# A fused attention and MLP kernel: near keys first, summary keys in rows 96 to 119, and V's means by products for pairs 0 and 1

## The chip, the cores and the metric

The kernel runs on one core of a Trainium2 chip. The metric is the device time of one execution in microseconds (us); the profile of one execution gives the span from the first to the last instruction. Engines are named as in the profile: PE (TensorE matmul), PEld (its weight loads), DVE (VectorE), ACT (ScalarE), POOL (GpSimd), and SP, on whose queue every DMA is issued.

## The reference, cut to what matters

Two batches, 8 heads, 768 positions, head size 64. Each query attends to keys less than 16 positions away and to 24 summary keys, one for each block of 32 positions; the output feeds two MLP layers.

```python
k_sum = k.reshape(B, H, nb, block, D).max(axis=3)       # block = 32, nb = 24
v_sum = v.reshape(B, H, nb, block, D).mean(axis=3)
mask_l = np.abs(pos[:, None] - pos[None, :]) < window   # window = 16
scores_s = scale * np.einsum('bhsd,bhnd->bhsn', q, k_sum) + np.log(block)
a = softmax(concatenate([where(mask_l, scores_l, -1e9), scores_s]))
x = a @ concatenate([v, v_sum])
h = relu(x @ w_in); u, v = halves of h; v_n = normalise(v)
x = (u * (w_spatial @ v_n + b_spatial)) @ w_out
h = relu(x @ w_in2); out = (h * sigmoid(conv3(h))) @ w_out2
```

## The kernel before

Heads go in pairs: 8 pairs, numbered 0 to 7 (0 to 3 are batch 0). A pair's 768 queries are 12 blocks of 64, and six blocks make a group, so there are 16 groups, two to a pair. A block sees 94 near keys (`WK`, 64 and 15 on each side) and 24 summary keys, `NK` = 118 columns; the summaries stand in columns and rows 0 to 23, the near keys behind them.

A group goes through these steps, by function and line. `keys` copies scaled near keys into `kws` (`win`, L393/L395, one for each group), takes block maxima on DVE (`top`, L403, two halves for pairs 0 to 3) and puts them beside the near keys (`put`, L409). `group` writes logarithms, masks and scores into PSUM (`qk`, L483, L489, L499), takes the row maximum on DVE (L503), six exponentials on ACT (`exps`, L509), sum and reciprocal on DVE (L512, L515), normalises on POOL or DVE (L518), transposes three blocks at a time on PE (L522, two halves h0 and h1, copied by L545), multiplies by V (`pv`, L528) and writes two parts of the result (L550, L551). Two score buffers alternate, so the scores of group i+2 wait for the exponentials of group i. The result of `pv` and the transpose in `means` share the bank `xp`.

`means` gives the 24 means of V for a pair, into rows 0 to 23 of the V tile `vws` for all blocks (`put`, L455 on ACT, L457 on POOL or DVE). For pairs 0 and 2 (`MEANS_F`, `MEANS_PE`) they come from 24 products of the V windows with a matrix of 1/32 (L424), which needs zeros in rows 0 to 23 first (L828). For the other pairs V is loaded a second time in another layout (L377, 384 KB), summed on DVE (L445) and transposed on PE (L448).

The matmuls of the dense layers (`mm3`, three products for each, L310 to L312) fill PE between and after the groups. The order of all work is written out by hand: each `add` makes a numbered unit with a cost and its readers and writers, `ORDER` lists the unit numbers, two characters each, in the order of issue, and `PICK` names the engine of each unit that has a choice. Each engine and the SP queue run their units in that order. Where the planner's costs leave PE a gap of 0.5 us or more before the dense stage, it puts in fill matmuls on constants (`warm`, L768); `WARM` of them also stand at the start.

The first DMAs in the queue before are, in order: keys of pair 0 (two halves), queries of pair 0 (first half), keys of pair 1 (two halves), a part of w_in, queries of pair 0 (second half), another part of w_in, queries of pair 1 (first half), V windows of group 0, keys of pair 2 (first half), queries of pair 1 (second half), keys of pair 2 (second half), V windows of group 1. PE's order before, with qk, T (transposes), pv and the group's number: qk0, 6 fill, qk1, 5 fill, qk2, means of pair 0 (first 12 products), qk3, T0h0, means of pair 0 (last 12), T0h1, qk4, T1h0, pv0, T1h1, qk5, T2h0, pv1, qk6, T2h1, means of pair 1 (transpose), dense, T3h0, qk7, T3h1, pv2, T4h0, means of pair 2 (24 products), T4h1, and so on.

Of the kernel before, what the change touches and what calls it, by code (L numbers as in the profile page):

```python
# [11 lines left out]
F32 = mybir.dt.float32  # L12
# [13 lines left out]
WK = QB + 2 * HK  # L26
VK = QB + 32
NS = S // 32
NK = WK + NS
GB = 6  # L30
GA = GB // 2
NG = NB // GB
MK = 5 * WK + 2 * QB + GA * NS
DIRECT = ()
MEANS_F = (0,2)
# [7 lines left out]
MEANS_PE = (0,2)  # L43
# [11 lines left out]
    "AAABACADAGAjAEAhAFAHAkAiAIAlArAMBZANBbBcBaATAsAUAJA4BdAVAWAXA5AaAbAOAYAtBjAcAdAeAfAgAuAKAmBFAvAwBkCUA6A7APA8BGCVCTCSCWAL"  # L55
    "A9BwBxAxAyB9DKBHBlBmAnAoApBnAzAZBoCcB+A0DLDMCdByA+DIAqAQA1A-BeBABBBzDJA2A3B0B1BICpBSCqB-CeCfARCgC2CAChBpBCBDBEDSBqBrBsBf"
    "DxCrDTCsEhCtBgEfB2B3BTDfDgBhCECFBiCuB4B5BtBuBvCiCjBLBMEiBJCXDUDVDhBKCYBNCZBOBPBUCGBVBWCkASClB6B7CaCHCIB8DWC3EoEpCvCwEgCJ"
    "CbDXBQDsCmCnEqCBDNCxE1BXCyBRDYCoCzDyDZDaDiCCEVDjEUFPC0C1DtDkFOCDCLDOE2DbDlDBC4DPDQCKDzBYDuDmDnFNFQDRErEsEtDcEjFWDdC6C7De"
    "C8C9C+DoEuDpDqDrE3FjE4EvEwEkCMC-DACND0DvDCD1COCPCQDwFkFlFwFCFDC5D7D8D9D2D+D-DDF7F8DEDFDGCRDHD3GnGlFmExFnFXD4D5E5D6EFEGEH"
    "EIF9EAE6F+GmEYEaElGoEZEJFGEbEcFYFHFIFJEBECEDEmFKEdFZEEE7E8EPEQERESEnGRFLEeETFMGEGFGSEyE9EWFRFaEzEKELGGHSEMENHTF0GTF1FbE+"  # L60
    "FcE0E-FxGuG7GHF2F3F4EOHIGeFEGfFdFeHJFAGgGhGiFBF5FSGjF6GkHKHLFoG8GvGIGJHUFTFfFpHMHcFVFUHVHWHdHeHNHOHmFqFrHnEXFgHXGUFFGwG9"
    "FsF-FhFyHYHZGxGKHoFiHpJ6HPGyHqGLHfGVGWFtGMHgIjH6FuGNHwGXG+FvGAHhHrHaGzHxHyHzGYGZGBGDGCGOH7H8HQHRH0GaGPGQGbG0GpHsIuH9G-Gc"
    "GdGqG1G2HtHAHuHiIOG3FzIPIQGrGsHBG4HCIzHDLVI0I1IkHbH+GtH1G5G6HEHFHGJ9LOH2HvH-H3HjHkHHIvHlIbITIEIAIUIBICIlIeIfIJImInIRH4H5"
    "IoISIgJwIKIVIhILIwIMJSJTLQLPIcIDIYIdIWIXIZINIaIFIGIHIIIpJUJVIxI4IqI5LcJIJcI2JdI+I3JJLRIrIsI6I7ItJeJfI-IiI8JKJLJWJXJMJNJ7"
    "KIJAI9JgJhJOJPJBJCJDJEJFJmKcKdKeKfKgIyJQJRJnJxJiJjJyJoKhJzKJJpJGJHJqJYJZLSKwKmKSJ0KnJrJsK6K7J1JkJlKxJ+J8LEJ-KyKALFKzKBKT"
    "JaJtLTJbJuJ2J3LXJ4LUJvLWLjLYKCKKK8LZLeLaJ5KiLbKjLdLqKLKoLfLgKULGKpKDKELlKFKMLhLiLkKVKWKXKYKNKOKZKqK0LmKaLnKPM2K9K+LHKbK-"
# [11 lines left out]
)  # L78
PICK = (
    "001111110101011000111110111000000011000001101110001001000011111011000011000101010010101110011001001101001000011011100121"  # L80
    "0210001000100001102200001000010101000100000010000000000000000000000000200200200000200200200200"
)
WARM = 9

# [840 lines left out]
```

## Time and profile before

| what | value |
|---|---|
| median of 3 runs | 333.08 us (332.96 to 333.38) |
| the profiled execution | 333.22 us |
| its span | 331.4 us (1.8 us lie around it) |
| PE busy | 325.2 us, 98% of the span |
| DVE, ACT, POOL busy | 237.1, 186.2, 62.8 us |

Busy time of PE is no measure of its use alone, because the ends of matmuls are modelled; starts are recorded, so the distance from one start to the next tells what PE did.

### The profile page before, as it was taken

The numbers are of one execution on the slowest core, as the hardware profiler recorded it, in microseconds if no ns is written. First come the engines' busy times: TensorE is split into PE (matmuls) and PEld (weight loads), VectorE is DVE, ScalarE is ACT, GpSimd is POOL, SyncE is SP. The second block draws the span as 40 slices with busy tenths as digits, with TensorE's granted clock in tenths as the row PEclk, the third lists the DMA queues.
The fourth block names the chain that finished last, engine by engine and source line by source line (L and its number), as shares of the span: only waits on it lengthen the run. The fifth ranks groups of instructions, "written<-read, shape, count | busy, mean of one in ns | idle before, by whom it ended". The sixth has DMA issues, their size and how long they took to land.

```text
span 331.4 us, 6183 instructions
## 1 busy us (share of the span) xinstructions
PE 325.2 (98%) x2388; PEld 269.0 (81%) x2388; DVE 237.1 (72%) x453; ACT 186.2 (56%) x460; POOL 62.8 (19%) x84
## 2 busy tenths in 40 slices
PE   7999999999999999999999999999999999999996
PEld 3678788878788888889988888888888888888886
DVE  8998888887781457889998597899897975480000
ACT  3988879957533643434441465867877854460111
POOL 6695944533112053001000100000000000000000
PEclk9999999999999999999999999999999999999999
DMA  7998697542046600232523230330000000000101
GB/s 234 312 277 273 181 270 256 163 121 66 7 128 200 199 0 0 65 127 76 161 83 119 73 101 26 128 110 19 0 2 32 32 34 32 32 32 34 63 32 65
DMA packets 13325, 34.49 MB, mean 104 GB/s; under 512 B 1648, under 2 KB 3952, under 8 KB 13296
## 3 DMA queue, kind: packets, MB, share of 16 engines
q1 hardware_dynamic: 13296, 34.10, 32.6%
q8 instruction: 19, 0.31, 0.4%
q14 instruction: 10, 0.08, 0.1%
HBM read 30.95 MB, written 3.15 MB: 103 GB/s over the span
## 4 chain that ended last, share of the span: by engine, by line
PE 94%; DVE 3%; POOL 1%; issue 1%; ACT 1%; DVEq 0%; ACTq 0%; POOLq 0%
PE late L310 12%; PE late L311 12%; PE late L312 12%; PE mm L310 9%; PE mm L311 9%; PE mm L312 9%; PE xp L528 4%; PE pt L522 4%; PE xp L310 3%; PE xp L311 3%; PE xp L312 3%; PE pt L312 3%; PE pt L311 3%; PE pt L310 3%; PE s L499 2%; PE mm L424 1%
## 5 line engine op out<-in xcount | busy, mean ns | idle before, releaser
L716 DVE SCALAR_TENSOR_TENSOR v<-v,conv_t 128x767 f32<-128x767 f32 x32 | 32.5, 1016 | 10.9 <-ACT v L713 10.5
L509 ACT ACTIVATE a<-s,a 128x118 f32<-128x118 f32 x96 | 33.1, 387 | 1.9 <-DVE a L503 1.8
L294 ACT ACTIVATE a<-a 128x512 f32<-128x512 f32 (+1 forms) x28 | 17.7, 640 | 16.2 <-DVE w L279 7.1
L509 ACT ACTIVATION_READ_ACCUMULATOR a<-s,a 128x1 f32 x96 | 22.5, 234 | 0.0
L299 DVE SCALAR_TENSOR_TENSOR a<-a,a 128x512 uint32<-128x512 uint32 (+1 forms) x32 | 19.9, 621 | 2.7 <-ACT a L294 1.2
L518 POOL TENSOR_TENSOR a<-a,a 128x708 f32<-128x708 f32 x14 | 19.1, 1367 | 12.5 <-ACT tmp L589 8.1
L301 DVE SCALAR_TENSOR_TENSOR a<-a,a 128x512 uint32<-128x512 uint32 (+1 forms) x32 | 20.0, 624 | 1.1
L310 PE MATMUL late<-xh,a 128*128 128x512 f32 x48 | 18.7, 389 | 0.0
L311 PE MATMUL late<-xl,a 128*128 128x512 f32 x48 | 18.7, 389 | 0.0
L312 PE MATMUL late<-xh,a 128*128 128x512 f32 x48 | 18.7, 389 | 0.0
L719 ACT ACTIVATE v<-v 128x768 f32<-128x768 f32 x16 | 13.5, 843 | 9.1 <-DVE v L716 9.1
L722 DVE TENSOR_TENSOR v<-v 128x768 f32<-128x768 f32 x16 | 15.1, 955 | 3.3 <-ACT v L719 2.9
L522 PE MATMUL pt<-ident,a 128*118 128x128 f32 x96 | 16.7, 282 | 0.5 <-POOL a L518 0.4
L757 ACT COPY tmp<-late 128x512 f32<-128x512 f32 x7 | 4.1, 589 | 23.0 <-PE late L312 23.0
L279 POOL TENSOR_TENSOR w<-a,w 128x256 fp32r<-128x256 f32 (+1 forms) x11 | 9.6, 881 | 33.5 <-ACT w L285 33.3
L713 ACT ACTIVATE v<-v,conv_t 128x768 f32<-128x768 f32 x16 | 15.0, 940 | 0.6 <-DVE w L279 0.2
L528 PEld LDWEIGHTS xp<-a,a 118*64 118x64 f32 x384 | 12.5, 137 | 3.5 <-issue 2.4
L545 ACT COPY a<-pt 118x384 f32<-118x384 f32 x22 | 10.6, 481 | 7.7 <-PE pt L522 7.4
L503 DVE TENSOR_REDUCE a<-s 128x6 f32<-128x708 f32 x16 | 13.9, 880 | 1.4 <-PE s L499 1.2
L528 PE MATMUL xp<-a,a 118*64 118x64 f32 x384 | 14.7, 226 | 0.0
L310 PE MATMUL mm<-xh,w 128*128 128x256 f32 (+1 forms) x40 | 14.3, 358 | 0.0
L522 PEld LDWEIGHTS pt<-ident,a 128*118 128x118 f32 x96 | 10.5, 136 | 4.6 <-issue 1.2
(337 smaller groups left out, 1016.3 us busy)
## 6 DMA issues: line engine op xcount, KB each, us to landing
a<-w_in SPq DMA_DIRECT2D x12, 512.0 KB, 3.6
a<-w_out SPq DMA_DIRECT2D x8, 512.0 KB, 3.6
out<-tmp SPq DMA_DIRECT2D x11, 256.0 KB, 2.0
a<-vwin SPq DMA_DIRECT2D x8, 288.0 KB, 6.0
a<-v_in SPq DMA_DIRECT2D x6, 384.0 KB, 5.9
a<-vwin SPq DMA_DIRECT2D x4, 576.0 KB, 6.1
tmp<-w_spT SPq DMA_DIRECT2D x6, 384.0 KB, 3.6
a<-w_in SPq DMA_DIRECT2D x8, 256.0 KB, 5.4
```

Source lines behind the costliest of these rows:

```text
L294: mul = {"ACT": (0.2 + n / 1080, lambda: ACT.mul(fu.f(), half(1).bitcast(F32), 2.0 ** -112)), "POOL": (0.12 + n / 1050, lambda: POOL.tenso ...
L299: add({"DVE": (0.16 + n / 960, lambda: DVE.scalar_tensor_tensor(out=last.u(), in0=fu.u(), scalar=0x80000000, in1=last.u(), op0=ALU.bitwise ...
L301: add({"DVE": (0.16 + n / 960, lambda: DVE.scalar_tensor_tensor(out=fu.u(), in0=fu.u(), scalar=3, in1=last.u(), op0=ALU.logical_shift_left ...
L310: PE.matmul(ps, lhsT=lh, rhs=rh, start=first and i == 0, stop=False)
L311: PE.matmul(ps, lhsT=lh, rhs=rl, start=False, stop=False)
L312: PE.matmul(ps, lhsT=ll, rhs=rh, start=False, stop=last and i == n - 1)
L509: ACT.activation(out=e[:, u, :NK], in_=sv[:, u // GA, u % GA], func=AF.Exp, bias=st[:, 0, u:u + 1], scale=SCALE if direct else 1.0, accum_ ...
L518: eng.tensor_tensor(out=e, in0=e, in1=st[:, 1].unsqueeze(2).to_broadcast([128, GB, NK]), op=ALU.mult)
L522: PE.transpose(pt3[:NK, a], e[:, GA * h + a, :NK], ident)
L528: PE.matmul(po[h * D:(h + 1) * D, k * QB:(k + 1) * QB], lhsT=vw3(j)[:NK, g * GB + k, h * D:(h + 1) * D], rhs=pts[:NK, at:at + QB], start=T ...
L716: DVE.scalar_tensor_tensor(out=ct.f()[:, to], in0=hh.f()[:, of], scalar=conv_t[:, 3 * f + k:3 * f + k + 1], in1=ct.f()[:, to], op0=ALU.mul ...
L722: eng.tensor_tensor(out=ct.f(), in0=hh.f(), in1=ct.f(), op=ALU.mult)
```

## The change

The columns and rows are turned round: near keys in 0 to 95 (`WK` becomes 96, two of them zero and masked), summaries in 96 to 119, so `NK` is 120. Key DMAs bring 800 columns for 798, in cuts of 416 and 384. The products for the means read rows 0 to 95 alone, so the zeros (L828) and the second way by a matrix `comb` (L826) go. Pairs 0 and 1 now take their means by products; pair 2 loads V again, and sums and transposes it as pairs 3 to 7 do. The logarithm is spread over 64 rows (`ones` on the left), which drops the constants `three` and `many`; inner masks are one tile read three times. The tile `one` is made on ACT (`one_tile`) and no longer on DVE. Planner costs change, `WARM` is 7, and `ORDER` and `PICK` are new.

By the new tables PE has as many units as before (515), ACT 286 for 281, DVE 393 for 399, POOL 74 for 74. The first DMAs are: keys of pair 0 (second half, then first), a part of w_in, queries of pair 0 (first half), keys of pair 1 (two halves), queries of pair 0 (second half), another part of w_in, queries of pair 1 (first half), V windows of group 0, keys of pair 2 (two halves), queries of pair 1 (second half), V windows of group 1. PE's order is: qk0, 3 fill, qk1, 7 fill, qk2, means of pair 0 (first 12), qk3, T0h0, means of pair 0 (last 12), T0h1, qk4, T1h0, pv0, qk5, T1h1, means of pair 1 (24 products), T2h0, pv1, T2h1, qk6, T3h0, pv2, T3h1, qk7, T4h0, pv3, two dense units, T4h1, means of pair 2 (transpose), qk8, T5h0, pv4, T5h1, T6h0, pv5. Both orders have done the same work at the end of T8h1. PE changes its way of tiling 50 times before and 51 times after.

```diff
-WK = QB + 2 * HK
-VK = QB + 32
+WK = QB + 32
-MEANS_F = (0,2)
+MEANS_F = (0,1)
-MEANS_PE = (0,2)
-WARM = 9
+WARM = 7
...
-            dma((k1 - k0) / 2, lambda k0=k0, k1=k1: SP.dma_start(kt(n).ap[:, k0:k1], k_in[b, p][:, k0:k1]), r - 12 + 0.5 * i, writes=[kt(n).tok(k0, k1)])
+            dma((k1 - k0) / 2 * (1.07 if kp == 2 else 1.0) - (90 if n + i == 0 else 0), lambda k0=k0, k1=k1: SP.dma_start(kts[n % 2].ap[:, k0:k1], k_in[b, p][:, k0:k1]), r - 12 + 0.5 * i, writes=[kts[n % 2].tok(k0, k1)])
...
-            dma(48 * (b1 - b0), lambda b0=b0, b1=b1: SP.dma_start(vw3(j)[NS:NS + VK, b0:b1], vwin[b, p][:, b0:b1]), r - 6 + 0.5 * i,
+            dma(52 * (b1 - b0), lambda b0=b0, b1=b1: SP.dma_start(vw3(j)[:WK, b0:b1], vwin[b, p][:, b0:b1]), r - 6 + 0.5 * i,
...
-                dst = kw3(j)[:, g * GB:(g + 1) * GB, NS:]
+                dst = kw3(j)[:, g * GB:(g + 1) * GB, :WK]
...
-                        PE.matmul(ps, lhsT=runs_t.ap[:NK, NZ - 2 * blk:NZ - 2 * blk + NS], rhs=vw3(j)[:NK, blk], start=blk == 0, stop=blk == NB - 1)
-                add({"PE": (1.41, mm)}, r + 1 + 0.5 * g, [vw_tok(j, g, "w"), vw_tok(j, g, "m"), runs_t.tok()], [m], mode="F")
+                        PE.matmul(ps, lhsT=runs_t.ap[:WK, NZ - 2 * blk:NZ - 2 * blk + NS], rhs=vw3(j)[:WK, blk], start=blk == 0, stop=blk == NB - 1)
+                add({"PE": (1.41, mm)}, r + 1 + 0.5 * g, [vw_tok(j, g, "w"), runs_t.tok()], [m], mode="F")
...
-                dst, src = vw3(j)[:NS, g * GB:(g + 1) * GB], vss[j].ap[:NS].unsqueeze(1).to_broadcast([NS, GB, 128])
+                dst, src = vw3(j)[WK:NK, g * GB:(g + 1) * GB], vss[j].ap[WK:NK].unsqueeze(1).to_broadcast([NS, GB, 128])
...
-                    PE.matmul(sv[c * QB:(c + 1) * QB, h, :, :NS], lhsT=(many if direct else three)[rows], rhs=logs[rows].rearrange("p (a k) -> p a k", k=NS),
+                    PE.matmul(sv[c * QB:(c + 1) * QB, h, :, WK:], lhsT=ones[rows, :QB], rhs=logs[rows].rearrange("p (a k) -> p a k", k=NS),
...
+    def one_tile():
+        for h, rows in enumerate(halves):
+            ACT.copy(one[rows], ident[rows, h * QB:(h + 1) * QB])
     def mask_tiles():
-        for h, rows in enumerate(halves):
-            DVE.tensor_copy(one[rows], ident[rows, h * QB:(h + 1) * QB])
         DVE.tensor_copy(tiles[:, 0], tiles[:, 1])
-        DVE.tensor_copy(tiles[:, 2:], tiles[:, 1].unsqueeze(1).to_broadcast([128, 3, WK]))
+        DVE.tensor_copy(tiles[:, 2:], tiles[:, 1].unsqueeze(1).to_broadcast([128, 2, WK]))
...
-    add({"DVE": (0.2, lambda: DVE.tensor_reduce(out=comb.ap, in_=ident.rearrange("p (j r) -> p r j", r=32)[:, :NS], op=ALU.add, axis=AX.X))}, -97, [tok("ident")], [comb.tok()])
-    for j in sorted({n % 2 for n in MEANS_PE}):
-        add({"POOL": (1.4, lambda j=j: POOL.memset(vws[j].ap[:NS], 0.0)), "DVE": (0.85, lambda j=j: DVE.memset(vws[j].ap[:NS], 0.0))}, -98, writes=[vws[j].tok(sub="m")], lock=True)
+    add({"ACT": (2.65, one_tile)}, -99, [tok("ident")], [mask_b.tok(sub="o")])
+    add({"DVE": (0.55, mask_tiles)}, -99, [tok("ident")], [mask_b.tok(sub="m")], lock=True)
```

## Rows read from the trace of the kernel before

**Rows 1.** The page: busy shares in 40 slices of 8.3 us.
```profile
PE   7999999999999999999999999999999999999996
```

**Rows 2.** Busy time by stage; ends with clock, DMA share and GB/s.
```profile
8.00:20.00 12.00, 11.55 (x207) 8.02 (x209) 10.92 (x25) 10.51 (x53) 8.65 (x12) 1.00 1.05 312
```

**Rows 3.** The timeline of the first 14 us, the start; start, duration, engine, line.
```profile
2.79 1.37 POOL L828 MEMSET a<- 24x1536 f32 x1
2.99 1.44 DVE L798 CAST a<-ident 64x64 bf16<-64x64 f32 x2
...
5.25 0.53 DVE L403 TENSOR_REDUCE a<-a 128x12 f32<-128x384 f32 x1
...
5.92 0.67 ACT L393 ACTIVATE a<-a 128x564 f32<-128x564 f32 x1 [2.12 <-DMA a<-k_in]
6.50 0.31 DVE L409 TENSOR_SCALAR a<-a 128x288 f32<-128x288 f32 x1
...
7.00 0.43 SPq L371 DMA_DIRECT2D a<-q_in  x1
7.13 0.45 ACT L294 ACTIVATE a<-a 128x256 f32<-128x256 f32 x1 [0.53 <-DMA a<-w_in]
```

**Rows 4.** PE's timeline from 5 to 60 us, the first groups.
```profile
6.91 0.84 PE L499 MATMUL s<-a,a 64*64 64x118 f32 x24 [1.32 <-DVE a L409]
...
13.45 0.23 PE L483 MATMUL s<-a 64*64 64x72 bf16 x4
...
14.85 0.54 PE L522 MATMUL pt<-ident,a 128*118 128x128 f32 x3 [0.45 <-POOL a L518]
15.32 1.49 PE L424 MATMUL mm<-a,a 118*24 118x128 f32 x12
...
23.02 0.54 PE L522 MATMUL pt<-ident,a 128*118 128x128 f32 x3
23.65 0.28 PE L448 MATMUL xp<-ident,a 128*24 128x128 f32 x1
```

**Rows 5.** ACT's timeline: exponentials of groups 0, 1, 2 and 6, first of each.
```profile
8.73 0.36 ACT L509 ACTIVATE a<-s,a 128x118 f32<-128x118 f32 x1 [1.16 <-DVE a L503]
...
11.04 0.36 ACT L509 ACTIVATE a<-s,a 128x118 f32<-128x118 f32 x1
...
13.62 0.39 ACT L509 ACTIVATE a<-s,a 128x118 f32<-128x118 f32 x1
...
27.00 0.37 ACT L509 ACTIVATE a<-s,a 128x118 f32<-128x118 f32 x1
```

**Rows 6.** DMA issues of the queries, line L371.
```profile
DMA to landing us min/median/max: 3.7/5.8/8.2
```

**Rows 7.** The chain that ended last, 18 to 30 us: start, duration, what.
```profile
23.04 0.57 DVE xl L551
...
24.17 0.11 PE mm L312
...
24.37 0.52 PE pt L522 x3
24.89 0.16 PE s L483 x4
...
25.19 0.31 PE s L489 x4
25.51 0.60 PE s L499 x24
...
26.58 0.85 PE xp L528 x24
```

**Rows 8.** POOL's timeline: normalising and putting.
```profile
21.69 2.69 POOL L518 TENSOR_TENSOR a<-a,a 128x708 f32<-128x708 f32 x2
24.36 0.65 POOL L395 TENSOR_SCALAR a<-a 128x564 f32<-128x564 f32 x1
...
33.03 0.82 POOL L457 TENSOR_SCALAR a<-a 24x768 f32<-24x768 f32 x1
```

More of the change, by code (lines that the diff above doesn't have):

```diff
@@ L186, in u, with bf16_parts @@
         return self.ap.bitcast(U32)
-def bf16_parts(x, k):
-    out, kind = [], mybir.dt.np(BF16)
-    for _ in range(k):
+def bf16_parts(x, times):
+    kind = mybir.dt.np(BF16)
+    out = [float(np.float32(x / times).astype(kind))]
+    x -= times * out[0]
+    for _ in range(2):
         out.append(float(np.float32(x).astype(kind)))
-        x = np.float32(x) - np.float32(out[-1])
+        x -= out[-1]
     return out
@@ L408, in put @@
         def put(eng):
-            eng.tensor_scalar(out=kw3(j)[:, :, :NS], in0=ks.ap[:, :NS].unsqueeze(1).to_broadcast([128, NB, NS]), scalar1=SCALE, scalar2=0.0,
+            eng.tensor_scalar(out=kw3(j)[:, :, WK:], in0=ks.ap[:, :NS].unsqueeze(1).to_broadcast([128, NB, NS]), scalar1=SCALE, scalar2=0.0,
                               op0=ALU.mult, op1=ALU.add)
-        if n not in DIRECT:
-            add({"POOL": (0.44, lambda: put(POOL)), "DVE": (0.33, lambda: put(DVE))} if n else {"DVE": (0.33, lambda: put(DVE))}, r - 3, [ks.tok()], [kws[j].tok(sub="s")], lock=True)
+        add({"POOL": (0.44, lambda: put(POOL)), "DVE": (0.33, lambda: put(DVE))} if n else {"DVE": (0.33, lambda: put(DVE))}, r - 3, [ks.tok()], [kws[j].tok(sub="s")], lock=True)
     def means(n):
@@ L487, in qk @@
                 for h in range(2):
                     rows = slice(h * D, (h + 1) * D)
-                    PE.matmul(sv[c * QB:(c + 1) * QB, h, :, NS:], lhsT=one[rows], rhs=masks[rows].rearrange("p (t k) -> p t k", k=WK)[:, at:at + GA],
-                              start=False, stop=True, skip_group_check=True)
+                    rhs = tiles[rows, 1].unsqueeze(1).to_broadcast([D, GA, WK]) if not first and not last else tiles[rows, int(last):int(last) + GA]
+                    PE.matmul(sv[c * QB:(c + 1) * QB, h, :, :WK], lhsT=one[rows], rhs=rhs, start=False, stop=True, skip_group_check=True)
@@ L491, in qk @@
             for a in range(GA):
-                for part in (0, 1) if direct else (2,):
-                    for c in range(2):
-                        blk = g * GB + 2 * a + c
-                        for h in range(2):
-                            rows = slice(h * D, (h + 1) * D)
-                            k0, k1 = ((NS, NK), (0, NS), (0, NK))[part]
-                            rhs = (kt_.ap[rows, blk * QB:blk * QB + WK], ks.ap[rows, :NS], kws[j].ap[rows, blk * NK:(blk + 1) * NK])[part]
-                            PE.matmul(s[c * QB:(c + 1) * QB, h, a * NK + k0:a * NK + k1], lhsT=qts[j].ap[rows, blk * QB:(blk + 1) * QB],
-                                      rhs=rhs, start=False, stop=True, skip_group_check=True)
+                for c in range(2):
+                    blk = g * GB + 2 * a + c
+                    for h in range(2):
+                        rows = slice(h * D, (h + 1) * D)
+                        PE.matmul(sv[c * QB:(c + 1) * QB, h, a], lhsT=qts[j].ap[rows, blk * QB:(blk + 1) * QB], rhs=kws[j].ap[rows, blk * NK:(blk + 1) * NK],
+                                  start=False, stop=True, skip_group_check=True)
```

146 lines of the change are left out of this document (60 added, 86 removed).

## The prediction

> **What bounds the kernel now.** I read the page first. Its slices show PE at nine tenths or more from the second slice to the last but one [rows 1], so outside the start and the end only a change in PE's work, or in the gaps between it, moves the time. That busy share has modelled ends, so I then took PE's timeline and went by starts. The first scores of keys begin at 6.91, after PE had waited 1.32 us for a DVE operation; at 14.85 PE has waited 0.45 us for POOL [rows 4]. The chain of waits between 18 and 30 us shows the small gaps that follow [rows 7]. After about 45 us I find hardly a gap in the starts, and the dense layers are the same in both kernels. So the question is what the first 45 us, the stage of the groups, give or take; at the end of T8h1 both orders have done the same PE work, and a lead there is a lead at the end.
>
> Around the start I read what makes PE wait. DVE's two casts for the tile `one` (64x64 elements each) take 1.44 us together, beginning in the POOL memset of the zero rows (2.79 to 4.16) and ending just after it at 4.43; the maxima and `put` (L409, 6.50) come behind them [rows 3]. From 8 to 20 us the DMA engines are full (share 1.05, 312 GB/s), with DVE busy for 10.92 and ACT for 10.51 of 12 us [rows 2]. What lands when is therefore set by how many bytes were queued ahead.
>
> **The start of the changed kernel.** The memset goes, the casts go to ACT (idle then: its first row here waits 2.12 us for a DMA), and the sum for `comb` goes. From the end of the POOL constants at about 2.8, DVE has mask copies (between the casts' end at 4.43 and the first maximum at 5.25 they took 0.8), two maxima of 0.53 and a `put` of 0.31 [rows 3], so summary keys are ready at about 5.0, against 6.81 before. But the first half of the queries is now the fourth DMA, behind a part of w_in: 848 KB. The fourth DMA before (798 KB, keys of pair 1) let ACT go at 5.92 [rows 3], so the queries land at about 6.1. First scores: 6.1 for 6.91, a lead of 0.8.
>
> Should ACT's two casts take as long as DVE's did, they would end by about 4, still ahead of the queries.
>
> **Where the lead goes.** Exponentials of group 0 begin when ACT has done the near keys of pair 1, which need the sixth DMA. The sixth DMA before (w_in, 1246 KB) let ACT go at 7.13; now it is the second half of the keys (1247 KB), so 7.1 + 0.67 = 7.8, and the exponentials start at 7.9 for 8.73 and those of group 1 at 7.9 + 2.3 = 10.2 for 11.04 (2.3 is the distance of these two rows) [rows 3, 5]. They end at about 12.4. Then ACT's queue has the near keys of pair 2, second group, in front of the exponentials of group 2, and these need the twelfth DMA. The twelfth before was queries, issued at 7.00 [rows 3] and landing 5.8 later by the median [rows 6], at 12.8; the bytes ahead are the same. So group 2's exponentials start at 12.8 + 0.7 = 13.5, for 13.62 [rows 5]. Likewise qk3 needs the second half of the queries of pair 1, now the thirteenth DMA: 192 KB at 312 GB/s [rows 2] is 0.6, so 13.4, for 13.45 [rows 4]. At qk3 the lead is 0.05: the keys moved ahead of the queries give it back. Bounds: if DMAs land no later than others need them, qk3 starts after the exponentials of group 1 at 12.4, 1.05 earlier; if they land 0.5 later than these medians, 0.5 later.
>
> **What is saved behind qk3.** The waits of PE that the new order has no cause for:
> - T0h0: POOL's normalising of group 0 ended just before 14.85, long after the exponentials (11.04 at the latest), since DVE and POOL did a weight conversion first. In the new order its sum stands before the maxima of group 2, ready by 13.3, while qk3 ends at 14.3. Gain 0.45 [rows 4].
> - The transpose for pair 1's means waited for the bank `xp`, until DVE's copy ended at 23.61. T2h1 began at 23.02 and three transposes take 0.47 (14.85 to 15.32), so 0.16 was lost [rows 4, 7]. Pair 1 has products now. Pair 2's transpose comes after two dense units and T4h1, which cover the same copies. Gain 0.16.
> - T3h0 waited for POOL until its second normalising ended at 24.38: dense work ended at 24.28, T3h0 began at 24.37. The mask writes of qk7 waited until 25.19, while logarithms had ended at 25.05 and POOL's near keys ended at 25.01 [rows 7, 8]. Together 0.25. In the new order 24 products of pair 1 (two times 1.4) stand before T2h0, so PE asks for both later, by about the time of the products less what stood there.
> Sum 0.86; by starts instead of modelled ends it would be up to 1.2. I take 1.0.
>
> **What is added on PE.** Scores have 120 columns for 118: 2/118 of 0.60 for each of 16 groups is 0.16 [rows 7]. Mask writes grow from 282 to 288 columns: 2% of 0.31, 16 times, at most 0.1, and parts of the array overlap in them, so 0.04. One more change of tiling; three transposes are 0.47 before another tiling, and a change costs between 0 and 0.1 [rows 4]: I take 0.1. Transposes (120 for 118 columns of weights) and `pv` keep their streamed columns, 128 and 64: I take nothing; at most 2/118 of 0.47 for each of 32 sets, 0.25 [rows 4]. Products of means: same number and columns, 96 rows for 118, so nothing; if rows counted, 22/118 of a set of twelve (1.49 at most [rows 4]) would be won four times, 1.1. Nothing in the rows goes by rows of weights (a product with 118 rows takes 0.12, a transpose with 128 rows and the same columns 0.16), so it stays a bound. Exponentials and maxima grow 1.7%: 0.04 a group on ACT, under the DMA waits above. DVE's sum for pair 1 and the second load of V (384 KB) move to pair 2: they leave the full stretch before 20 us for one that is less full, which can only help early; late they stand under PE's products.
>
> For the transposes there is a rule that speaks against the change. The Trainium skill, "TensorE: Matmul & The Clock Gate", section "LDWEIGHTS (loading the stationary operand)", has a weight load take its number of columns over 1.2 in ns, whatever the rows. An estimate from that page: 96 loads with two more columns are 0.16 us, if nothing hid them, and the sum would be 332.5 (rival 4). No row here shows a load of 120 columns.
>
> Sum: -0.05 - 1.0 + 0.16 + 0.04 + 0.1 = -0.75 on the profiled execution's 333.22 (span 331.4), so 332.47. That execution lies 0.14 above the median of 333.08, so 332.3.
>
> **Rivals.**
> 1. *The waits are not gone but moved (no change).* ACT, DVE and POOL are as full as PE in this stage [rows 2], and 24 products early leave fewer later to fill with. If half of the 1.0 comes back as other gaps, the time is 332.8. For it: POOL and DVE have their queues full of conversions, as before. Against: the gaps of before each have a named cause that is out of the way. A measurement of this kernel can tell about 0.2% (0.67 us) from no change.
> 2. *Slower: POOL behind the means of pair 2.* They come only after T4h1, at about 31.3: to qk3's 13.4 come five scores of 0.9 (mask writes at 25.19 to 26.11), ten sets of transposes of 0.47, four `pv` of 0.85, 36 products of 0.12 (one set: 1.42 before the next unit), and two dense units of 1.1, three times 0.12 and three times about 0.24; 17.9 in all [rows 4, 7]. Then 0.3 to copy, 0.82 to put them (L457) and 1.37 to normalise group 6 behind that, in this order on POOL [rows 8]: ready at 33.8 to 34.1. PE asks for T6h0 after the transpose 0.2, qk8 0.9, T5h0 0.47, pv4 0.85 and T5h1 0.47 [rows 4, 7], at 34.2. The slack is 0.1 to 0.4. Group 6's exponentials start about 28.2 in the new queue (two copies and a result stand before them) for 27.00 [rows 5]; they are no limit. Should POOL be one normalising (1.35) later, PE loses 1.2 here, and group 7 behind it some more: 333.5 to 333.9. It decides from a lateness of about 1 on, which takes the gain away.
> 3. *The whole lead survives.* If key and query DMAs land up to 1.05 before these medians, the 0.8 of the start is kept: 332.3 - 0.9 = 331.4. For it: the key buffers of pair 0 come free before DVE's old 6.5, so the queue can be filled earlier [rows 3]. Against: the engines are full anyway [rows 2].
> 4. *The wider transposes show.* If the two columns lengthen each set of transposes by the bound above, 0.25, and nothing else differs, the time is 332.6. For it: sets follow one another with little PE work between. Against: 128 columns stream over weights of either width.
>
> **How the numbers follow.** Forecast (gaps go, start given back) 0.40, at 332.3; rival 3, 0.15, at 331.4; rival 1, 0.22, at 332.8; rival 4, 0.05, at 332.6; rival 2, 0.18, at 333.7. The limit for faster is 332.41: rival 3, most of the forecast and a little of rival 1 give faster 0.55; rival 4, the rest of 1 and some of the forecast give same 0.28; rival 2 but for its smallest cases gives slower 0.17. The range runs from rival 3 with the bound of its DMAs, 331.2, to rival 2, 333.7; the forecast's own is 331.8 to 332.8.
>
> **What would show it.** First scores at about 6.1 and exponentials of group 0 at 7.9; group 2's exponentials no earlier than 13.3; no wait of PE for POOL near T0h0; T8h1's end earlier by 0.7 to 1.0; PE without gaps between 31 and 36. A first score later than 6.6, a gap before T6h0, or new gaps in the dense stage after 45 us would make it wrong.

## The result, and the profile after

The changed kernel takes **335.0 us** (median of 6, 334.50 to 335.21) against 333.12 before (332.83 to 333.38): a ratio of 1.0057, interval 1.0046 to 1.0067. It is slower by 1.9 us where 0.8 us less was forecast, and it lies outside the predicted range. The profiled execution took 334.95 us with a span of 333.2 (before 333.22 and 331.4).

The page's PE slices of the changed kernel look as full as those of before [rows 1], with one tenth less in one slice, the seventh (50 to 58 us):

```profile
PE   7999998999999999999999999999999999999996
```

So I go by starts again, in PE's timeline of the changed kernel (start, us, engine, line, operation, tile, and in brackets the idle time before it and what ended it):

```profile
6.76 0.84 PE L474 MATMUL s<-a,a 64*64 64x120 f32 x24 [0.95 <-DMA a<-q_in]
...
13.14 0.23 PE L461 MATMUL s<-a,ones 64*64 64x72 bf16 x4
...
14.04 0.54 PE L495 MATMUL pt<-ident,a 128*120 128x128 f32 x3
14.51 1.49 PE L417 MATMUL mm<-a,a 96*24 96x128 f32 x12
...
34.94 0.51 PE L495 MATMUL pt<-ident,a 128*120 128x128 f32 x3 [0.74 <-ACT a L517]
...
44.77 0.54 PE L495 MATMUL pt<-ident,a 128*120 128x128 f32 x3
...
54.77 0.39 PE L311 MATMUL mm<-xh,w 128*128 128x512 f32 x1
56.63 0.39 PE L309 MATMUL mm<-xh,w 128*128 128x256 f32 x1 [1.47 <-ACT v L584]
```

The same point of both orders, T8h1, where all work of the groups up to there is done alike, starts at 44.77 here and at 44.95 before:

```profile
44.95 0.54 PE L522 MATMUL pt<-ident,a 128*118 128x128 f32 x3
```

The lead at T0h0 is 0.81 (14.04 for 14.85, and no wait there [rows 4]); 0.18 of it is left at T8h1. From T8h1 to the end of the span it takes 288.43 us (333.2 less 44.77) for 286.45 before: **2.0 us are lost behind T8h1**, where I had called both kernels the same. The one long wait of PE there stands at 56.63. The dense matmul before it started at 54.77 and its like follow at distances of 0.23, so PE lost 1.63 us. It waited for a bank that the relu (L584) empties on ACT. ACT's timeline shows why the relu was late:

```profile
50.67 0.60 ACT L584 ACTIVATE v<-mm 128x512 f32<-128x512 f32 x1 [0.36 <-PE mm L311]
53.58 0.68 ACT L293 ACTIVATE a<-a 128x512 f32<-128x512 f32 x1 [2.31 <-DMA a<-w_in]
54.16 0.35 ACT L482 ACTIVATE a<-s,a 128x120 f32<-128x120 f32 x1
...
56.17 0.41 ACT L584 ACTIVATE v<-mm 128x256 f32<-128x256 f32 x1
```

Behind one relu stands a multiply of a weight conversion (L293), which waited 2.31 us for its load of w_in, then six exponentials, then the next relu. That relu does not need the load; it only stands behind it. The Trainium skill, "PSUM — Partial Sum Buffer", section "Engine vs sequencer instructions", calls ScalarE's queue strictly first in, first out, and this row agrees. Before, the multiply stood in front of a relu too, but waited 0.36, and no exponentials stood between:

```profile
52.59 0.68 ACT L294 ACTIVATE a<-a 128x512 f32<-128x512 f32 x1 [0.36 <-DMA a<-w_in]
53.18 0.36 ACT L612 ACTIVATE v<-mm 128x256 f32<-128x256 f32 x1
```

And the load was late because of the queue that issues it. These are a row of the SP queue's waits (us in total, times, longest), two of its timeline, and two windows of the changed kernel (busy time of PE, PEld, DVE, ACT, POOL with instructions, granted clock, DMA share, GB/s):

```profile
SPq L365 <- PE s L474: 6.2, 1, 6.2
```
```profile
37.74 0.33 SPq L365 DMA_DIRECT2D a<-q_in  x1
...
45.41 0.35 SPq L292 DMA_DIRECT2D a<-w_in  x1
```
```profile
36.00:38.50 2.50, 2.50 (x53) 2.02 (x48) 2.36 (x6) 2.46 (x11) 1.18 (x3) 1.00 0.12 32
40.00:53.00 13.00, 13.00 (x165) 11.22 (x154) 10.61 (x24) 9.95 (x37) 5.82 (x9) 1.00 0.97 266
```

The queries of pair 6 wait 6.2 us in the queue for scores of PE that free their buffer. In that time nothing behind them is issued, and the DMA engines fall to a share of 0.12. What was held back then comes all at once: from 40 to 53 us they are full (0.97), and the w_in that ACT wants lands 8 us after its issue at 45.41. In the kernel before, the same two windows have shares of 0.83 and 0.85, and all its queries together waited 0.3 us for scores:

```profile
SPq L371 <- PE s L499: 0.3, 1, 0.3
```

### The profile page after: what moved, and what is told of

Its sections match the earlier page's. It is cut to its first block, busy times and chain, and to the rows that moved or that the text cites. A ratio compares the mean times of both kernels' runs of the same rounds, so it can differ in the third digit from the quotient of the medians.

```text
span 333.2 us, 6182 instructions
## 1 busy us (share of the span) xinstructions
PE 325.7 (98%) x2389; PEld 269.2 (81%) x2389; DVE 236.5 (71%) x437; ACT 191.0 (57%) x466; POOL 61.6 (18%) x84
## 4 chain that ended last, share of the span: by engine, by line
PE 92%; DMA 4%; ACT 2%; DVE 1%; SPq 0%; issue 0%; ACTq 0%
PE late L309 12%; PE late L310 12%; PE late L311 12%; PE mm L309 9%; PE mm L311 8%; PE mm L310 8%; PE xp L501 4%; PE pt L495 3%; PE xp L310 3%; PE xp L309 3%; PE xp L311 3%; PE pt L309 3%; PE pt L310 3%; PE pt L311 3%; PE s L474 2%; DMA a<-w_in 2%
## 5 line engine op out<-in xcount | busy, mean ns | idle before, releaser
L482 ACT ACTIVATE a<-s,a 128x120 f32<-128x120 f32 x96 | 33.1, 389 | 0.2 <-DVE a L478 0.2
L293 ACT ACTIVATE a<-a 128x512 f32<-128x512 f32 (+1 forms) x27 | 17.4, 643 | 16.1 <-DVE w L278 4.7
L278 POOL TENSOR_TENSOR w<-a,w 128x256 fp32r<-128x256 f32 (+1 forms) x13 | 12.3, 947 | 44.7 <-ACT w L284 44.0
L491 POOL TENSOR_TENSOR a<-a,a 128x720 f32<-128x720 f32 x12 | 16.6, 1391 | 16.1 <-DVE a L488 16.0
L495 PE MATMUL pt<-ident,a 128*120 128x128 f32 x96 | 16.6, 281 | 0.9 <-ACT a L517 0.7
L296 DVE TENSOR_SCALAR a<-a 128x512 uint32<-128x512 uint32 (+1 forms) x32 | 14.4, 450 | 3.1 <-DMA a<-w_in 2.9
L309 PE MATMUL mm<-xh,w 128*128 128x512 f32 (+1 forms) x40 | 14.6, 366 | 1.5 <-ACT v L584 1.5
L501 PEld LDWEIGHTS xp<-a,a 120*64 120x64 f32 x384 | 12.5, 137 | 3.6 <-issue 2.3
L478 DVE TENSOR_REDUCE a<-s 128x6 f32<-128x720 f32 x16 | 14.4, 904 | 1.3 <-PE s L474 1.1
L569 POOL TENSOR_TENSOR stat<-stat,mhalf 128x1 f32<-128x1 f32 x12 | 8.3, 702 | 35.6 <-DVE stat L566 35.5
L501 PE MATMUL xp<-a,a 120*64 120x64 f32 x384 | 14.7, 226 | 0.1
## 6 DMA issues: line engine op xcount, KB each, us to landing
a<-vwin SPq DMA_DIRECT2D x8, 288.0 KB, 6.8
```

Source lines behind the costliest of these rows:

```text
L293: mul = {"ACT": (0.2 + n / 1080, lambda: ACT.mul(fu.f(), half(1).bitcast(F32), 2.0 ** -112)), "POOL": (0.18 + n / 1050, lambda: POOL.tenso ...
L309: PE.matmul(ps, lhsT=lh, rhs=rh, start=first and i == 0, stop=False)
L482: ACT.activation(out=e[:, u, :NK], in_=sv[:, u // GA, u % GA], func=AF.Exp, bias=st[:, 0, u:u + 1], accum_out=sm[:, u, :1])
L491: eng.tensor_tensor(out=e, in0=e, in1=st[:, 1].unsqueeze(2).to_broadcast([128, GB, NK]), op=ALU.mult)
L495: PE.transpose(pt3[:NK, a], e[:, GA * h + a, :NK], ident)
L501: PE.matmul(po[h * D:(h + 1) * D, k * QB:(k + 1) * QB], lhsT=vw3(j)[:NK, g * GB + k, h * D:(h + 1) * D], rhs=pts[:NK, at:at + QB], start=T ...
```

## The experiments

Each changes the hand-written order, named here by its unit numbers, or goes part of the way back. "To the end" is the span less the start of T8h1 in the profiled execution; it leaves out what happens before that point. Spans are read to 0.1 us, so it is good to about 0.1. The ratio is to executions of the kernel before that ran beside each kernel (medians 332.86 to 332.97); the kernels ran on more than one chip, so ratios compare better than medians.

| kernel | median us | ratio to before | span | T8h1 | to the end |
|---|---|---|---|---|---|
| before | 333.12 | | 331.4 | 44.95 | 286.45 |
| changed | 335.0 | 1.0057 (1.0046 to 1.0067) | 333.2 | 44.77 | 288.43 |
| relu first | 334.05 | 1.0022 (1.0008 to 1.0037) | 332.8 | 45.16 | 287.64 |
| loads first | 333.7 | 1.0023 (1.0012 to 1.0034) | 331.8 | 45.15 | 286.65 |
| scores early | 334.14 | 1.0037 (1.0017 to 1.0057) | 331.5 | 44.84 | 286.66 |
| layout, old order | 333.13 | 0.9997 (0.9986 to 1.0008) | 331.4 | 44.88 | 286.52 |
| all moves | 333.48 | 1.0012 (0.9996 to 1.0028) | 331.2 | 44.50 | 286.70 |
| load later | 338.41 | 1.0158 (1.0126 to 1.0191) | 334.4 | 44.76 | 289.64 |
| queries first | 334.18 | 1.0032 (1.0016 to 1.0048) | 333.2 | 46.55 | 286.65 |
| vector too | 334.45 | 1.0036 (1.0019 to 1.0052) | 332.5 | 45.67 | 286.83 |
| normalise first | 333.37 | 1.0013 (1.0004 to 1.0021) | 331.9 | 44.99 | 286.91 |
| load much later | 341.38 | 1.0259 (1.0245 to 1.0272) | 339.5 | 44.86 | 294.64 |
| changed again | 335.97 | 1.0100 (1.0082 to 1.0118) | 332.8 | 44.80 | 288.0 |
| two more | 333.85 | 1.0022 (1.0006 to 1.0037) | 333.4 | 45.20 | 288.2 |

My theory was that ACT's queue behind a late load costs the time. The rival was that the new layout itself is dearer on PE; a second rival put the loss down to the earlier gap at T6h0.

**Relu first.** The waiting relu goes ahead of the multiply in ACT's queue.

```diff
-280 312 344 313 314 281 255 256 356 264
+264 280 312 344 313 314 281 255 256 356
```

Here 264 is the relu, 280 the multiply and 281 DVE's shift of the same load.

> One move in the changed kernel's order: the relu of f1u's tile (f 2, 256 columns) comes ahead of ScalarE's multiply for the first 512-column piece of w_in, and nothing else. In the changed kernel PE waited 1.47 us at 56.63 for that relu (starts 54.78 to 56.63, 1.6 more than two such products need), and ScalarE had stood 2.31 us before that multiply for the load of w_in. Theory A (the loss is ScalarE's queue held by a late load): the stall of PE before that product falls under 0.3, the load still lands at about 53.5, and the time is 335.0 - 1.4 = 333.6 (333.2 to 334.0). Theory B (the wider columns and the extra products make the whole stage slower, and the stall only shows where PE first runs ahead): the same time is lost in other gaps before 70 us and the time stays above 334.5.

PE's wait of 1.47 us is gone; "to the end" falls by 0.8. The median, 334.05, lies just above the expected range. ACT's multiply still waits 1.06 for the load, now with the relu done:

```profile
52.47 0.38 ACT L584 ACTIVATE v<-mm 128x256 f32<-128x256 f32 x1 [0.83 <-PE mm L311]
...
53.92 0.68 ACT L293 ACTIVATE a<-a 128x512 f32<-128x512 f32 x1 [1.06 <-DMA a<-w_in]
```

Only 0.8 of the 2.0 us came back, because DVE has the same load in its own queue. Its shift waits, the conversion's steps follow, and the summary keys of pair 6 (L403), which PE's next scores need, stand behind them; PE then waits for these:

```profile
53.83 0.43 DVE L296 TENSOR_SCALAR a<-a 128x512 uint32<-128x512 uint32 x1 [1.60 <-DMA a<-w_in]
...
56.83 0.30 DVE L403 TENSOR_SCALAR a<-a 128x288 f32<-128x288 f32 x1
```
```profile
57.19 0.84 PE L474 MATMUL s<-a,a 64*64 64x120 f32 x24 [0.46 <-DVE a L403]
```

**Loads first.** ACT's and DVE's queues stay as they are; two other loads (a part of w_in, V of pair 4) are put on the SP queue ahead of the queries that wait 6.2 us, into the stretch where the DMA engines stood at 0.12. The load that ACT waits for keeps its place in the queue.

```diff
-322 192 204 277 296 133 132 134 135 136 183
+192 183 322 204 277 296 133 132 134 135 136
```

> Only the DMA queue's order is changed: the second part of w_in for pair 3 and the values of pair 4 are issued ahead of the queries of pair 6. In the changed kernel these queries' issue waited 6.2 us for the scores at 36.9 to 37.7, and the DMA engines moved only 14 to 105 GB/s from about 35.7 to 38.3. Theory A: those 2.5 us of transfers move into the hole, the first 512-column piece of w_in lands by 51.5 to 52.5 instead of 53.47, ScalarE's wait before its multiply falls from 2.31 to about 1 and PE's wait at 56.63 from 1.47 to 0.5 or less: 333.6 to 334.2. Theory A with another cause of the lateness (the engines are full from 40 to 53 us whatever comes before): it lands at 53.2 to 53.5 and the time stays at 334.8 to 335.1. Theory B: no change whatever lands when.

The DMA engines' share from 36 to 38.5 us is 1.02 here instead of 0.12, and 0.80 instead of 0.97 from 40 to 53. The load that ACT wants is issued no earlier (45.78 for 45.41), but in ACT's timeline the same multiply now starts at once, 2.06 earlier than in the changed kernel, and the relu behind it is in time; in PE's the dense matmuls run through at the usual distance:

```profile
51.52 0.67 ACT L293 ACTIVATE a<-a 128x512 f32<-128x512 f32 x1
...
54.12 0.41 ACT L584 ACTIVATE v<-mm 128x256 f32<-128x256 f32 x1
```
```profile
55.13 0.39 PE L311 MATMUL mm<-xh,w 128*128 128x512 f32 x1
55.36 0.28 PE L309 MATMUL mm<-xh,w 128*128 128x256 f32 x1
```

"To the end" is 286.65, within 0.2 of before. The late load, through what stands behind it, makes 1.8 of the 2.0 us. The gap of 0.74 at T6h0 is still there in this kernel, so the second rival falls: that gap is not what costs the time behind T8h1. The median falls by 1.3, from 335.0 to 333.7.

**Scores early.** With the relu first as well, the scores of the ninth group (308) go ahead of T6h0 (215), so that PE has work while ACT empties the transposes' bank, and a dense unit (236) goes ahead of T7h0 (228).

```diff
-176 177 215
+176 177 308 215
...
-217 308
+217
...
-228 229 236
+236 228 229
...
-280 312 344 313 314 281 255 256 356 264
+264 280 312 344 313 314 281 255 256 356
```

> The move of the first of these kernels (relu ahead of the multiply), and with it two moves on PE: the scores of group 9 stand between the second transposes of group 5 and the first of group 6 (where PE waited 0.74 us for the copy out of the one transpose bank), and a 512-column unit of f1u ahead of the first transposes of group 7. Theory A: the wait before T6h0 goes, the queries of pair 6 are issued some 2.5 us earlier since their buffer is read by group 9's scores, and a gap of 0.3 to 0.8 comes back before the second transposes of group 7, which need ScalarE's and VectorE's copies one after the other: 333.0 to 333.6, no more than 0.5 below the first kernel. Theory B: as the first kernel, over 334.5.

The gap of 0.74 at T6h0 is gone, and parts of it come back as two smaller ones, of 0.3 and 0.2; the third row below is a wait of 0.16 at T5h0 that the changed kernel has too. These are all of PE's waits from 30 to 110 us (us in total, times, longest):

```profile
PE xp L427 <- DVE xl L523: 0.3, 1, 0.3
PE s L461 <- ACT a L482: 0.2, 1, 0.2
PE pt L495 <- DVE a L485: 0.2, 1, 0.2
```

T8h1 starts at 44.84, no earlier than with the gap; counted from T0h0, which came 0.22 later in this execution, 0.15 of the 0.74 is won. But "to the end" is as good as with the loads first: the queries' issue, which waits for those same scores, came at 35.40 instead of 37.74. This is the late load's cause from its other side, though with the relu moved as well. The median, 334.14, is above the expected 333.0 to 333.6.

**Layout with the old order.** The rows, columns and operations of the changed kernel, but means by products for pairs 0 and 2, and with `ORDER`, `PICK` and the fills of before (the numbers of the fills are written in).

```diff
-MEANS_F = (0,1)
+MEANS_F = (0,2)
-WARM = 7
+WARM = 9
...
-                if self.fill and gap >= 0.5:
-                    n = int((gap - 0.1) / 0.22)
+                n = {42: 2, 55: 6, 98: 5}.get(k, 0)
+                if self.fill and n:
```

> The change's layout alone in the order of the kernel before: near keys in 0 to 95, summary keys in 96 to 119, no zeros, the casts for `one` on ScalarE; but means by products for pairs 0 and 2, and every unit at its old place in every queue (same warm-up products as before). My working priced the layout at +0.2 (scores and mask writes) and gave the start's lead back at the scores of group 3: 333.3 (332.9 to 333.6). Theory A: no slower than that, since the stall of the dense stage belongs to the new order. Theory B (the layout itself costs): 334 or more, with the loss spread over the 16 groups.

Its time is that of before within an interval of -0.14% to +0.08%: a cost of the layout, if there is one, is too small to see here, and the loss of 1.9 us is not the layout's. PE's timeline shows the same point again and again: a lead that is given back.

```profile
5.89 0.84 PE L474 MATMUL s<-a,a 64*64 64x120 f32 x24
9.19 0.85 PE L474 MATMUL s<-a,a 64*64 64x120 f32 x24 [0.77 <-DMA a<-q_in]
11.33 0.79 PE L474 MATMUL s<-a,a 64*64 64x120 f32 x24
14.90 0.54 PE L495 MATMUL pt<-ident,a 128*120 128x128 f32 x3 [0.34 <-POOL a L491]
...
44.88 0.54 PE L495 MATMUL pt<-ident,a 128*120 128x128 f32 x3
```

The first scores start 1.0 earlier than before (5.89 for 6.91 [rows 4]), with the memset, the sum for `comb` and DVE's casts gone. PE then waits 0.77 for queries, the scores of group 2 start at 11.33 (before at 11.32), and T0h0 waits for POOL again.

**All moves** of relu first, loads first and scores early on the new order, with the summary keys of pair 6 (381) ahead of DVE's shift (281).

```diff
-176 177 215
+176 177 308 215
...
-308 322 192 204
+192 183 322 204
...
-228 229 236
+236 228 229
...
-280 312 344 313 314 281
+264 280 312 344 313 314 381 281
```

> All moves that helped so far in one kernel: the relu ahead of ScalarE's multiply, the two loads ahead of the queries of pair 6, the scores of group 9 and a unit of f1u earlier on PE, and VectorE's summary keys of pair 6 ahead of its part of the same conversion. Theory A (the loss is in the order, by in-order queues behind a late load and by the one transpose bank): no PE wait over 0.3 us between 45 and 110 us, and a little below the kernels with one of these moves: 332.9 to 333.5, about the kernel before. Theory B' (about 0.3 us more is lost behind the second transposes of group 8 for other reasons, the wider scores among them): it can't come below 333.0.

Between 30 and 110 us PE has the three short waits of "scores early" and no other. The time, 333.48, is that of before within the interval; nothing is won.

**Load later.** The changed kernel, but the DMA that the multiply needs (279) is issued behind the next load of w_in (325).

```diff
-140 279 141
+140 141
...
-325 280
+325 279 280
```

> The suspected cost made larger, in the changed kernel itself: the DMA for the first 512-column piece of w_in is issued behind that for the second, which has to wait for VectorE's reads of the other buffer until about 48.5. Nothing else moves. Theory A: the piece lands at about 54.7 instead of 53.47, and PE's wait before the product at 56.6 grows by the same 1.2 us, from 1.47 to 2.7: 336.2 (335.8 to 336.6). Theory B: the time stays at 335.0, since the load is not what PE waits for.

ACT's multiply waits 1.23 longer, and PE waits 1.23 longer: one for one, as the theory says.

```profile
54.80 0.68 ACT L293 ACTIVATE a<-a 128x512 f32<-128x512 f32 x1 [3.54 <-DMA a<-w_in]
```
```profile
57.84 0.38 PE L309 MATMUL mm<-xh,w 128*128 128x256 f32 x1 [2.70 <-ACT v L584]
```

The profiled execution took 336.26, 1.3 above the changed one's. The five others, and with them the median, lie above the expected range: they took 337.85 to 340.19 with a mean granted clock of 0.995 to 0.989, where the profiled one had 0.999; where in them the clock fell was not recorded.

**Queries first.** "All moves", and the first queries of pair 0 (7) go ahead of a part of w_in (24), the second of pair 1 (14) ahead of keys of pair 2 (67).

```diff
-6 0 2 1 4 5 24 31 25 7
+6 0 2 1 4 5 7 24 31 25
...
-9 36 67 99
+9 36 14 67 99
```

> The kernel with all moves, and at the start the first half of the queries ahead of the first part of w_in, and the second half of the queries of pair 1 ahead of the keys of pair 2. My prediction's steps: first scores about 0.8 earlier than in the changed kernel (6.76), at 5.9; the scores of group 3 then wait for the exponentials of group 1 and not for their queries, so they start at 12.9 for 13.3, and T0h0 is earlier by 0.3 to 0.5. If a lead at T0h0 lasts, the time is 0.3 to 0.5 below the kernel with all moves: 332.4 to 333.0. Rival: any lead of the start is taken back in the next waits (exponentials of group 2, the transposes of group 6), and the two times are the same within 0.2.

A miss, for two reasons. The planner sets its fill matmuls by its own costs, and with this order it put 14 of them before the first scores (13 in the changed kernel) and none before those of group 1. In this execution they kept PE until about 6.9, so the first scores began at 7.03, without a wait for queries. The second reason is again a queue: the conversion's shift of w_in stands ahead of the first row maximum on DVE, so the load that now lands later holds up the exponentials of group 0 until 9.64 (8.61 in the changed kernel):

```profile
7.29 0.29 DVE L296 TENSOR_SCALAR a<-a 128x256 uint32<-128x256 uint32 x1 [2.26 <-DMA a<-w_in]
```

T0h0 came at 15.07 (14.04 in the changed kernel).

**Vector too.** Relu first on ACT, and the summary keys of pair 6 ahead of the shift on DVE, with the load at its place in the changed kernel's queue.

```diff
-280 312 344 313 314 281 255 256 356 264
+264 280 312 344 313 314 381 281 255 256 356
```

> The first kernel (relu ahead of the multiply) with one more move: VectorE's summary keys of pair 6 ahead of its part of the late conversion. With the relu alone the wait of 1.47 was gone, but the scores of group 12 came to wait 0.46 us for these summary keys, which stood on VectorE behind the same load (1.60 us of waiting at 53.83). Theory A: that wait goes as well, the load still lands at about 53.8 and what is left of the stall is under 0.4 in all: about 0.6 below the first kernel, 333.3 to 333.6. Rival: the conversion itself is needed by then (products of the dense stage read w_in's second half), and the wait moves on to them: no gain.

"To the end" falls to 286.83, and PE waits neither for the relu nor for the summary keys. How little a late load costs then is not shown, for the load was less late here: DVE's shift began 7.74 us behind T8h1 (53.41 less 45.67), for 8.73 in the changed kernel (53.50 less 44.77), and ACT's multiply had no wait. The median, 334.45, is above the expected 333.3 to 333.6 and no better than with the relu alone. In the profiled execution T8h1 already starts 0.9 late, since the scores of group 3 waited 0.68 for queries, though the order there is that of the changed kernel; how it was in the other executions is not recorded. Over the kernels with this start the first scores begin between 6.48 and 7.15, and T8h1 between 44.50 and 45.67.

**Normalise first.** Layout with the old order, but sum, reciprocal and normalising of group 0 ahead of a weight conversion on DVE and POOL.

```diff
-27 28 29 30 31 45 9 37 68 46 47
+45 46 27 28 29 47 30 31 9 37 68
```

> The layout in the old order once more, with one of the waits taken out that my prediction counted as saved (0.45 us before T0h0): VectorE's sum and reciprocal of group 0 and GpSimd's normalising stand ahead of the second part of w_in's conversion. Prediction's step (a wait removed from PE in this stage is a gain at the end): T0h0 starts right behind the scores of group 3, at about 14.5 for 14.9, and the time is 0.3 to 0.45 below the layout in the old order: 332.7 to 332.9. Rival (a lead in this stage is taken back at the next unit that waits for another engine or a load): T0h0 is earlier, but at the second transposes of group 8 nothing is left: within 0.15 of 333.1.

T0h0 starts 1.05 earlier and does not wait. Of this, 0.58 was there at the scores of group 3 (13.13 for 13.71), ahead of the wait that was removed. The next transposes wait 0.80 for DVE's copy, and at T8h1 (44.99) nothing is left. The time, 333.37, is above both forecasts; 0.4 us of it lie at 66.16, where 24 products of scores take 1.21 for 0.78 and the profile names no releaser. The rows are of this kernel:

```profile
13.85 0.54 PE L495 MATMUL pt<-ident,a 128*120 128x128 f32 x3
...
16.62 0.54 PE L495 MATMUL pt<-ident,a 128*120 128x128 f32 x3 [0.80 <-DVE a L517]
```

**Load much later.** As "load later", but behind keys, queries and V (367, 368, 323) too.

```diff
-140 279 141
+140 141
...
-325 280
+325 367 368 323 279 280
```

> The changed kernel with the DMA for the first 512-column piece of w_in issued behind the second piece, the keys and queries of pair 7 and the values of pair 6 (some 1.7 MB, at 250 to 290 GB/s about 6 us of transfers, part of which must wait for buffers). When the load stood 1.2 us later, the profiled execution had a wait of 2.7 us and took 336.26 us, as expected, but other executions took 337.9 to 340.2 with a mean granted clock of 0.989 to 0.995. Theory A alone: PE's wait grows to 6 or more and the time is 335.0 plus the growth, with a granted clock of 1.0 in every stretch. Theory A with a second cost (PE's clock falls to the lower level in or behind a long enough wait): the profile shows a stretch behind 55 us with a granted clock under 1, and the time is higher than the wait explains by 1 us or more.

PE's wait grows by 4.0 to 5.47, ACT's multiply having waited 6.31, and "to the end" grows by 6.2. The other 2.2 are the clock, which the windows show (columns as above), and PE's timeline with it: 24 products of scores take 1.41 for 0.79, and from the matmul that waited to the next product with V PE takes 4.90 us (60.71 to 65.61) for 2.65 in the changed kernel (56.63 to 59.28).

```profile
54.00:58.00 4.00, 1.24 (x6) 0.69 (x4) 0.43 (x1) 0.35 (x1) 0.00 (x0) 1.00 0.53 211
58.00:62.00 4.00, 1.29 (x6) 1.24 (x7) 3.60 (x8) 3.83 (x17) 0.00 (x0) 0.59 0.42 131
62.00:66.00 4.00, 4.00 (x79) 3.36 (x79) 2.59 (x5) 3.77 (x10) 2.73 (x3) 0.56 0.39 137
66.00:70.00 4.00, 4.00 (x40) 3.49 (x36) 3.86 (x7) 3.45 (x21) 2.14 (x4) 1.00 0.00 0
```
```profile
60.71 0.58 PE L309 MATMUL mm<-xh,w 128*128 128x256 f32 x1 [5.47 <-ACT v L584]
...
62.80 1.41 PE L474 MATMUL s<-a,a 64*64 64x120 f32 x24
```

**Changed again.** The changed kernel unaltered, on the chip of the last two runs.

> The changed kernel itself, unaltered, beside the same runs of the kernel before, to have the experiments' times against its own on this chip: 334.5 to 335.2 as before. The kernels with the moved relu or loads had times from 333.0 to 335.5, with first scores between 6.5 and 7.2 us in their profiles; if the start of this order depends on when the first loads land, this kernel's times should spread by 1 us or more as well when it is run more often.

It is slower again, and by more: 335.97, a ratio of 1.0100, above the time expected. Its six executions spread by 3.1 us (334.54 to 337.64), as expected by more than 1; the 17 of the kernel before beside them lie within 0.7. The profiled one is the fastest of the six. In it ACT's multiply waited 1.91 and PE 1.05 at the same matmul, each 0.4 less than in the first profile (2.31 and 1.47), and "to the end" is 0.4 less as well: one for one again, without any edit. What the five slower executions lost is not recorded.

**Two more.** "All moves", a dense unit (241) ahead of a transpose for means (205) on PE, and a copy out of the transposes' bank (164) ahead of the scaling of V's means (152, L429) on DVE.

```diff
-205 241
+241 205
-152 153 79 164
+164 152 153 79
```

> The kernel with all moves, with its two largest remaining gaps of PE between 30 and 40 us attacked as well: VectorE copies the second transposes of group 4 ahead of the means of pair 2 (T5h0 waited 0.16), and a 256-column unit of f1u stands ahead of the transpose for pair 3's means, which waited 0.31 for VectorE. If a gap removed here lasts to the end: 0.3 to 0.4 below the kernel with all moves, whose ratio to the kernel before was 1.0012: 332.4 to 333.2, a ratio of 0.9995 to 1.0005. Rival (what is gained at one wait is given back at the next): the same ratio as the kernel with all moves, within 0.0010.

A miss. The 0.3 ahead of the transpose for means went. POOL's put of V's means (L436), which needs the scaling now later, let `pv` of group 4 wait 0.47 at 33.42: near the place, and by the engine, of my rival 2. The profiled execution also has one pause of 1.44 us at 47.57, for which the profile names no releaser; no other kernel here shows it. Without it "to the end" would be 286.8.

## Why the prediction was wrong, step by step

**What failed is the step on what bounds the kernel**: "After about 45 us I find hardly a gap in the starts, and the dense layers are the same in both kernels. … a lead there is a lead at the end." A lead of 0.18 at T8h1 became a loss, for behind it 2.0 us went. In the kernel before, the multiply waited only 0.36 for its load, and the relu stood right behind it. The new order moves both: loads on SP stand behind queries that wait for PE, and a relu on ACT stands behind an operation that waits for such a load, with six exponentials more between. That this makes the loss is shown from three sides: with the relu moved PE's wait goes (relu first), with the load earlier it goes (loads first), and with the load later it grows one for one (load later). "Changed again" bears it out, with a load less late; "vector too" agrees, but with a load that was less late too. Of the 2.0 us behind T8h1, the load accounts for 1.8. Of the last 0.2 (286.65 to 286.70 against 286.45), 0.07 is there under the old order too (286.52); the rest I did not place, and it is near what the spans resolve. None of my rivals had a price for a loss behind 45 us; rival 2, which had one for a slower kernel, had another cause.

**First scores at 6.1**: 6.76. I took the landing from the bytes queued ahead, 848 KB beside a row with 798. In the changed kernel POOL's multiply (L294) was let go by the first part of w_in, the third DMA, only at 5.90, at the time at which 798 KB had landed before (5.92 [rows 3]). The lead was 0.15 and not 0.8. Why these bytes took longer is open.

**The start given back by qk3**: the lead at qk3 was small, as forecast, but not for the reason given. Exponentials of group 0 came at 8.61 for 7.9: I had counted one window of near keys on ACT before them, where two stood (1.26 us from 7.17), and the row maximum behind the late first scores ended later still. Those of group 1 came at 10.64 for 10.2, qk3 at 13.14 for 13.4: a lead of 0.31 for 0.05. PE shows no wait for queries there, the step by which I had the lead given back; it had hardly been there to begin with. Only in "vector too" did queries hold these scores, by 0.68. "Layout with the old order" does show a lead given back: 1.0 at the first scores is nothing at group 2.

**Waits saved behind qk3, 1.0**: T0h0 came without a wait, as forecast, and with 0.81 of lead, and from there to T5h0 (32.36) PE's timeline names no other. But two new waits came, 0.16 at T5h0 and 0.74 at T6h0, and by T8h1 0.18 was left. Rival 1, waits that move, describes what happened here. The gap of 0.74 stands in the place that rival 2 names, but has another cause. POOL was on time by rival 2's own sum: its two normalisings began at 32.70, so that of group 6 ended at about 34.1, within the 33.8 to 34.1 worked out there, when T5h1 had just left PE free. What PE waited for was ACT's copy out of the transposes' one bank, queued behind a put of 0.83 us:

```profile
32.70 2.74 POOL L491 TENSOR_TENSOR a<-a,a 128x720 f32<-128x720 f32 x2
```
```profile
33.46 0.83 ACT L434 COPY a<-a 24x768 f32<-24x768 f32 x1
34.31 0.48 ACT L517 COPY a<-pt 120x384 f32<-120x384 f32 x1
```

In the new order no PE work stands between T5h1 and T6h0 to cover it. "Normalise first", "scores early" and "two more" say the same: in this stage a wait that is taken away comes back at the next engine.

**What is added on PE**: small, and nothing for the transposes. "Layout with the old order" took 333.13, where I had counted 0.2 for scores and masks; its interval, -0.5 to +0.3 us, does not decide about them. The first rows are the changed kernel's (instructions by form; duration in ns, least, median and most), the second those of before:

```profile
L495 PEld LDWEIGHTS pt<-ident,a x96: 133/137/143, 14.0 to 99.2; 128*120 128x120 f32 x96
L495 PE MATMUL pt<-ident,a x96: 270/272/327, 14.0 to 99.3; 128*120 128x128 f32 x96
```
```profile
L522 PEld LDWEIGHTS pt<-ident,a x96: 133/136/143, 14.8 to 94.4; 128*118 128x118 f32 x96
L522 PE MATMUL pt<-ident,a x96: 270/272/328, 14.8 to 94.5; 128*118 128x128 f32 x96
```

A load of 120 columns takes 1 ns more by the median, a matmul as long as before (272 ns, about twice the load that runs beside it), and three of them still start 0.47 before the next unit (14.04 to 14.51). Rival 4 falls. By the rule of the Trainium skill that I weighed there ("TensorE: Matmul & The Clock Gate", section "LDWEIGHTS (loading the stationary operand)") an estimate is 98 and 100 ns for the two widths. These rows show 136 and 137, and the loads of 64 columns for `pv` in the same trace take 138 by the median, so the recorded times do not follow that rule here; the measurement decides. Rival 3, a lead that survives, falls too, with 0.18 left at T8h1. The list of what would make it wrong was better than the forecast: a first score later than 6.6, a gap before T6h0 and a new gap in the dense stage after 45 us all came.

## What to carry to other kernels

Before calling a later stage the same in two orders, look in each engine's queue for what stands behind an instruction that waits for a load, and in the DMA queue for what stands behind a transfer that waits for a buffer: here a conversion whose load was late held up a relu that PE needed at once. A load's order is as much a part of the change as its consumer's, and putting two loads before a transfer that waits took 1.8 us off the work behind T8h1. A lead won at the start of this stage, in which four engines are nearly full, was hardly a lead at its end (0.81 became 0.18, 1.0 became 0.07, 1.05 became nothing); follow it through every wait up to there before it is put into the sum.

## What the hardware showed that I had not expected

In and behind PE's wait of 5.47 us the granted clock was 0.59 and then 0.56 of full speed over 58 to 66 us, so at the lower level (1.2 of 2.4 GHz) for most of that time, and 1.00 again in the next window, after PE had been busy all through the one before: 2.2 us beyond the wait itself. In the profiled executions with waits of 1.47 and 2.70 at the same matmul, the granted clock was 1.00 from 54 to 62 us.

The start differs between executions. In the ten profiled ones with the same first DMAs, the first part of w_in let DVE go between 5.37 and 6.24 us, and the first scores began between 6.48 and 7.15. Not all of this is landings: PE's own 13 fill matmuls at the start took from 4.34 to 5.73 us, for which I have no cause, and in three of the ten no wait is shown before the first scores. Under the old order T8h1 starts within 0.11 (44.88 to 44.99) in three kernels whose first scores begin between 5.89 and 6.91. Whether the spread at the start is also what spreads the times of the new order is not shown, since only profiled executions have rows.
